# An attention and feed-forward kernel on one core: the first two batches by head pair, dense exponentials, quadrant kv, new weight layout

## The chip, the cores and the metric

The kernel runs on one core of one Trainium2 chip. Spans and instants come from one profiled execution per kernel and count from its first instruction. PE is TensorE (PEld its weight loads), ACT is ScalarE, DVE is VectorE, POOL is GpSimd, SP issues the DMAs.

## The reference

```python
# q, k, v: 8 batches x 8 heads x 576 x 64, f32
q_s = softmax(q, axis=-1)                 # over the 64 dimensions
k_s = softmax(k, axis=2)                  # over the 576 positions
kv  = einsum('bhsd,bhse->bhde', k_s, v)
att = einsum('bhsd,bhde->bhse', q_s, kv)
x   = att.transpose(0, 2, 1, 3).reshape(4608, 512)
h   = x @ w_in                            # 512 x 2048
g   = h * sigmoid(beta * h)
out = g @ w_out                           # 2048 x 512
```

## The kernel before

The work is cut into chunks, one per batch (512 rows) and one for the 64 last rows of all batches. Per chunk there are 16 groups `mm_a(c, j)` of four 128x512 matmuls (first product, followed by tanh on ACT and a multiplication on DVE) and 16 groups `mm_b(c, j)` of four (second product). Attention of a later batch is done beside the products of an earlier one. Batches 0 and 1 are special: batch 0 has nothing to hide behind, and batch 1's inputs come after all weights in the queue of loads. The program fixes the order of instructions on each engine, and each engine works in that order.

For batches 0 and 1 a tile of k holds a head pair, one head on partitions 0 to 63 and one on 64 to 127. `ek` was filled with zeros so that one 128x128 matmul does both heads:

```python
def kz_exp(b, j, m=1):
    for e in range(2):                      # two exps of 64 partitions each
        r = slice(e * D, (e + 1) * D)
        nc.scalar.activation(ek[b][r, j : j + m, :, e * D : (e + 1) * D],
                             k_st[b][r, j : j + m, :]..., ACTF.Exp)
# kv_mm: 9 matmuls per pair
nc.tensor.matmul(t[:, jl, 0:D1], ek[b][:, j, i, :], va[b][:, j, i, :], ...)

load_q(0, parts=2); load_kv(k_st, k, 0, "k_st", parts=4); load_kv(v_st, v, 0, "v_st", parts=4)
nc.sync.dma_start(beta_r[:], ...)
w_load("in", 0, 0); w_load("in", 0, 1); w_load("out", 0, 0); w_load("in", 1); w_load("out", 0, 1)
# ... rest of the weights, q of batch 1, then its k and v

# hand-over from batch 0 to batch 1, as emitted
for u in range(4, NJ):
    mm_a(0, u)                              # with exceptions at 4 and 5, cut
    mm_b(0, u - LAG)
    # ... q_exp, q_sum, q_mul, q_pet(1, 0 and 1) of batch 1 at u = 10 to 13, cut
    if u >= 12:
        kz_exp(1, u - 12)
for j in (2, 3):
    q_pet(1, j, nc.vector)                  # transposes of q on PE, copied out by DVE
mm_b(0, NJ - 2)
kv_mm(1, 0); kv_norm(1, 0)                  # two pairs in one PSUM tile
warm(2)
kv_mm(1, 1); kv_norm(1, 1)
mm_b(0, NJ - 1)
for j in range(HP):
    x_mm(1, j, nc.scalar if j % 2 == 0 else nc.vector, tag="h" if j < 2 else "att")
```

The softmax here doesn't subtract the row's maximum and nothing guards it: scores larger than these inputs give would overflow.

Of the kernel before, what the change touches and what calls it, by code (L numbers as in the profile page):

```python
# [17 lines left out]
def kernel(  # L18
# [40 lines left out]
    beta_r = const.tile([NJ, P], F32, name="beta_r")  # L59
    ident16 = const.tile([NJ, NJ], F32, name="ident16")  # L60
    w_in_b = const.tile([P, KT, FF], BF16, name="w_in_b")
# [11 lines left out]
    w_out_d = moe_w_out.rearrange("(j p) f -> p j f", p=P)  # L73
# [6 lines left out]
    def load_q(b, parts=1):  # L80
        t = stage.tile([P, H, R * D], F32, tag="q_st", bufs=2, name=f"q_st{b}")
        src = q[b, :, 0:MAIN, :].rearrange("h (p i) d -> p h (i d)", i=R)
        n = H // parts
        for s in range(parts):
            nc.sync.dma_start(t[:, s * n : (s + 1) * n, :], src[:, s * n : (s + 1) * n, :])  # L85
        q_st[b] = t
# [12 lines left out]
    def load_kv(d, src, b, tag, parts=1):  # L99
        t = stage.tile([P, H * (R + 1) * D], F32, tag=tag, bufs=2, name=f"{tag}{b}")  # L100
        if b < NW:
            d[b] = t[:, 0 : HP * RW * D].rearrange("p (j r) -> p j r", j=HP)
            sv = src[b].rearrange("(j e) (p i) d -> (e p) j (i d)", e=2, i=RW)
            n = HP // parts
            for s in range(parts):
                nc.sync.dma_start(d[b][:, s * n : (s + 1) * n, :], sv[:, s * n : (s + 1) * n, :])  # L106
# [11 lines left out]
    def w_load(kind, blk, half=None):  # L118
        if (kind, blk) not in wst:
            wst[kind, blk] = stage.tile([P, 4, 512], F32, tag="wo", bufs=4, name=f"w_{kind}{blk}")  # L120
        t = wst[kind, blk]
        if kind == "in":
            src = w_in_d[:, :, ds(blk * 512, 512)]
            c = slice(0, 512) if half is None else slice(half * 256, half * 256 + 256)
            nc.sync.dma_start(t[:, :, c], src[:, :, c])
        else:
            src = w_out_d[:, ds(4 * blk, 4), :]
            c = slice(0, 4) if half is None else slice(half * 2, half * 2 + 2)
            nc.sync.dma_start(t[:, c, :], src[:, c, :])

    def w_cast(kind, blk, half, eng):
        t = wst[kind, blk]
        if kind == "in":
            dst = w_in_b[:, :, ds(blk * 512 + half * 256, 256)]
# [12 lines left out]
    def ek_buf(b, eng=None):  # L147
        t = work.tile([P, HP * RW * P], BF16, tag="ek", bufs=2, name=f"ek{b}")
        if b < NW:
            ek[b] = t[:].rearrange("p (j i m) -> p j i m", j=HP, i=RW)  # L150
            eng.memset(t[:].bitcast(F32), 0.0)
# [3 lines left out]
    def kz_exp(b, j, m=1):  # L155
        for e in range(2):
            r = slice(e * D, (e + 1) * D)
            nc.scalar.activation(  # L158
                ek[b][r, j : j + m, :, e * D : (e + 1) * D],
                k_st[b][r, j : j + m, :].rearrange("p j (i d) -> p j i d", i=RW),  # L160
                ACTF.Exp,
            )
# [65 lines left out]
    def q_mul(b, s, n=2):  # L228
        m = H // n
        h = slice(s * m, (s + 1) * m)  # L230
        nc.vector.tensor_tensor(  # L231
# [25 lines left out]
    def kv_mm(b, jj, n=2, tag="att"):  # L257
        t = ps.tile([P, n, D1 if b < NW or COLT else 2 * D1], F32, tag=tag, bufs=2 if tag == "att" else 1, name=f"kv{b}_{jj}")
        att_of[b, jj] = t
        for jl in range(n):  # L260
            j = n * jj + jl
            if b < NW:
                for i in range(RW):
                    nc.tensor.matmul(  # L264
                        t[:, jl, 0:D1],
                        ek[b][:, j, i, :],
                        va[b][:, j, i, :],
                        start=(i == 0),
                        stop=(i == RW - 1),
                    )  # L270
# [80 lines left out]
    def mm_a(c, j, kts=None, tag=None):  # L351
# [103 lines left out]

    load_q(0, parts=2)
    load_kv(k_st, k, 0, "k_st", parts=4)
    load_kv(v_st, v, 0, "v_st", parts=4)
    nc.sync.dma_start(beta_r[:], moe_beta.rearrange("(j p) -> j p", p=P))
    w_load("in", 0, 0)  # L460
    w_load("in", 0, 1)
    w_load("out", 0, 0)
    w_load("in", 1)
    w_load("out", 0, 1)
    w_load("out", 1)
    w_load("in", 2)
    w_load("out", 2)
    w_load("in", 3)
    load_q(1, parts=2)
    w_load("out", 3, 0)  # L470
    load_kv(k_st, k, 1, "k_st", parts=4)
    w_load("out", 3, 1)
    load_kv(v_st, v, 1, "v_st", parts=2)
# [6 lines left out]
    make_identity(nc, ident16[:])  # L480
    ek_buf(0, nc.vector)
    nc.vector.memset(kvp[:, 0 : B - 1], 0.0)
    v_buf(0)
    ek_buf(1, nc.gpsimd)
# [17 lines left out]
    warm(18)  # L502
    for s in range(2):
        q_exp(0, s)
        q_sum(0, s)
        q_mul(0, s)
    for s in range(2):
        for j in (2 * s, 2 * s + 1):
            q_pet(0, j, nc.vector)
        warm(10 if s == 0 else 2)  # L510
    for j in range(HP):
        kz_exp(0, j)

    tb = ps.tile([P, 512], F32, tag="h", bufs=2, name="tb")

    def attn0(p):
        if 0 < p < 3:
            warm(1, tag="acc3")
        if p % 2 == 0:
            vz_cast(0, p, nc.gpsimd)  # L520
            vz_cast(0, p + 1, nc.gpsimd)
        kv_mm(0, p, n=1, tag=f"acc{p}")
        kv_norm(0, p, n=1)

    for p in range(HP):
        attn0(p)
        if p == 2:
            w_cast("in", 0, 0, nc.gpsimd)
        if p >= 1:
            x_mm(0, p - 1, nc.scalar)  # L530
        if p == 1:
            nc.tensor.transpose(tb[:, 0:NJ], beta_r[:], ident16[:])
            nc.scalar.copy(beta_t[:], tb[:, 0:NJ])
        if p >= 2:
            for j in range(2):
                mm_a(0, j, [p - 2])
    x_mm(0, HP - 1, nc.scalar)
    for kind, blk in (("in", 0), ("out", 0)):
        for half in range(2):
            if (kind, half) not in (("in", 0), ("out", 1)):  # L540
                w_cast(kind, blk, half, nc.gpsimd)
    for kt in (2, 3):
        for j in range(2):
            mm_a(0, j, [kt])
    w_cast("in", 1, 0, nc.vector)
    w_cast("in", 1, 1, nc.gpsimd)
    w_cast("out", 0, 1, nc.gpsimd)
    mm_a(0, 2)
    mm_a(0, 3)
    mm_b(0, 0)  # L550
    mm_b(0, 1)

    def pool_cast(*what):
        for kind, blk in what:
            for half in range(2):
                w_cast(kind, blk, half, nc.gpsimd)
# [6 lines left out]

    tail_zero(0)
    pool_cast(("out", 1), ("in", 2), ("out", 2))
    tail_zero(1)
    pool_cast(("in", 3), ("out", 3))

    for u in range(4, NJ):
        if u != 5:  # L570
            mm_a(0, u)
        if u == 4:
            mm_a(0, 5)
            mm_b(0, 2)
            continue
        if u == 13:
            for j in (0, 1):
                q_pet(1, j, nc.vector)
        mm_b(0, u - LAG)
        if u in (10, 11):  # L580
            q_exp(1, u - 10)
        if u in (10, 12):
            q_sum(1, (u - 10) // 2)
        if u in (11, 13):
            q_mul(1, (u - 11) // 2)
        if u >= 12:
# [12 lines left out]
    for j in range(HP):
        x_mm(1, j, nc.scalar if j % 2 == 0 else nc.vector, tag="h" if j < 2 else "att")  # L600
# [95 lines left out]
```

## Time and profile before

| | before |
|---|---|
| time, median | 289.15 us (288.61 to 289.18, 3 runs) |
| profiled span | 286.8 us |
| PE busy, granted clock | 97%, 1.000 |
| PE's stream of products from | 17.95 us (6 product matmuls done earlier) |
| waits in it up to the next line | 0.79 us, all before 39.02 us |
| end of batch 0's last first-product group | 42.92 us |
| first product of batch 1 | 48.75 us |
| from there to the end | 238.05 us |

The page's second part, each digit a fortieth of the span, shows PE near its limit everywhere but at both ends, at full clock:

```profile
PE   7799999999999999999999999999999999999994
...
PEclk9999999999999999999999999999999999999999
```

PE's timeline at the start (start, us, instruction, count, idle time before and who ended it). The first products (`h`) come two at a time between kv and x until 17.95 us. From there to 42.92 us PE has one gap, of 0.79 us read from start to start, ahead of the transposes of q at 39.02.

```profile
15.24 0.61 PE L358 MATMUL h<-xT,w_in_b 128*128 128x512 bf16 x2 [0.20 <-POOL w_in_b L145]
...
17.95 1.24 PE L358 MATMUL h<-xT,w_in_b 128*128 128x512 bf16 x5 [0.24 <-ACT xT L143]
...
39.02 0.61 PE L250 MATMUL tp<-identity,eq 128*128 128x128 bf16 x8 [0.62 <-ACT ek L158]
```

PE's timeline of the hand-over (start, us, instruction, count). A printed length includes a modelled drain of 0.17 us, so one reads from start to start: a group of four takes 0.863 us.

```profile
42.06 1.03 PE L358 MATMUL h<-xT,w_in_b 128*128 128x512 bf16 x4
42.92 1.03 PE L386 MATMUL acc<-w_out_b,g 128*128 128x512 bf16 x4
43.78 0.61 PE L250 MATMUL tp<-identity,eq 128*128 128x128 bf16 x8
44.23 1.03 PE L386 MATMUL acc<-w_out_b,g 128*128 128x512 bf16 x4
45.25 0.74 PE L264 MATMUL kv<-va,ek 128*128 128x65 bf16 x18
45.83 0.59 PE L450 MATMUL warm<-kvp 128*128 128x512 bf16 x2
46.26 0.74 PE L264 MATMUL kv<-va,ek 128*128 128x65 bf16 x18
46.84 1.03 PE L386 MATMUL acc<-w_out_b,g 128*128 128x512 bf16 x4
47.70 1.03 PE L314 MATMUL x<-qsT,kvp 128*128 128x512 bf16 x4
48.75 0.38 PE L358 MATMUL h<-xT,w_in_b 128*128 128x512 bf16 x1
```

### The profile page before, as it was taken

What the parts mean: (1) busy time and instruction counts of PE and PEld (TensorE: products, weight loads), DVE (VectorE), ACT (ScalarE), POOL (GpSimd) and SP (SyncE); (2) the same over time, 40 slices, a digit from 0 to 9 for tenths busy, and PEclk for the clock granted to TensorE, in tenths of its full rate; (3) what the DMA queues carried; (4) which work ended last, traced back from release to release, by engine and by line L of the source; (5) the groups of instructions that cost most, each with busy time, mean ns of one, the idle gap of its engine ahead of it and who ended that gap; (6) DMA issues with size and microseconds to landing.
All of it is one profiled execution on the core that took longest, in us unless ns stands there. A gap on an engine that the chain in (4) does not pass through costs nothing.

```text
span 286.8 us, 4132 instructions
## 1 busy us (share of the span) xinstructions
PE 277.9 (97%) x1595; PEld 127.7 (45%) x1595; DVE 180.0 (63%) x280; ACT 162.9 (57%) x236; POOL 43.7 (15%) x58
## 2 busy tenths in 40 slices
PE   7799999999999999999999999999999999999994
PEld 2444445444444444444444444444445444444441
DVE  7954597695477457855694469456954695464432
ACT  4763586683496448734773568356835563553341
POOL 4458833300030020001200030003000000000000
PEclk9999999999999999999999999999999999999999
DMA  7999999809933963296319911893270033005004
GB/s 242 377 385 387 371 388 321 280 2 264 280 151 76 313 164 146 46 331 175 127 33 270 269 74 76 194 268 119 115 220 2 1 149 73 0 0 149 0 0 146
DMA packets 56227, 50.08 MB, mean 175 GB/s; under 512 B 26240, under 2 KB 47760, under 8 KB 56208
## 3 DMA queue, kind: packets, MB, share of 16 engines
q1 hardware_dynamic: 56064, 49.56, 55.8%
q8 instruction: 12, 0.20, 0.3%
q10 hardware_dynamic: 144, 0.26, 0.3%
q14 instruction: 7, 0.06, 0.1%
HBM read 36.71 MB, written 9.44 MB: 161 GB/s over the span
## 4 chain that ended last, share of the span: by engine, by line
PE 84%; DMA 11%; SPq 1%; POOL 1%; ACT 1%; issue 0%; DVE 0%; ACTq 0%
PE acc L386 40%; PE h L358 39%; DMA w_in<-in_moe_w_in_dram 6%; DMA k_st<-in_k_dram 5%; PE x L314 2%; PE kv L276 2%; POOL w_in_b L145 1%; PE kv L264 0%; PE tp L250 0%; SPq L85 0%; SPq L106 0%; PE x L318 0%; ACT ek L158 0%; DVE g L370 0%; ACT th L368 0%
## 5 line engine op out<-in xcount | busy, mean ns | idle before, releaser
L368 ACT ACTIVATE th<-h,beta_t 128x512 bf16<-128x512 f32 x144 | 98.5, 687 | 102.6 <-PE h L358 100.7
L370 DVE SCALAR_TENSOR_TENSOR g<-th,h 128x512 bf16<-128x512 bf16 x144 | 97.9, 682 | 92.2 <-ACT th L368 90.7
L358 PE MATMUL h<-xT,w_in_b 128*128 128x512 bf16 x576 | 146.1, 379 | 0.5 <-ACT xT L143 0.2
L386 PE MATMUL acc<-w_out_b,g 128*128 128x512 bf16 x576 | 145.9, 379 | 0.2 <-DVE g L370 0.2
L386 PEld LDWEIGHTS <-g 128*128 128x128 bf16 x576 | 56.0, 98 | 67.9 <-DVE g L370 1.0
L358 PEld LDWEIGHTS <-w_in_b 128*128 128x128 bf16 x576 | 55.3, 98 | 67.7 <-issue 2.7
L145 POOL CAST va<-v_st 128x2048 bf16<-128x2048 f32 (+2 forms) x12 | 17.3, 1460 | 145.0 <-DMA v_st<-in_v_dram 145.0
L225 DVE TENSOR_REDUCE rq<-eq 128x16 f32<-128x1024 bf16 x18 | 21.6, 1198 | 2.3 <-ACT eq L214 2.3
L231 DVE TENSOR_TENSOR eq<-eq,rq 128x1024 bf16<-128x1024 bf16 x18 | 22.6, 1257 | 0.1
L214 ACT ACTIVATE eq<-q_st 128x1024 bf16<-128x1024 f32 x16 | 16.3, 1048 | 2.9 <-DMA q_st<-in_q_dram 2.9
L143 ACT CAST xT<-x 128x512 bf16<-128x512 f32 x20 | 11.6, 585 | 11.1 <-PE x L314 10.3
L169 ACT ACTIVATE ek<-k_st 128x1024 bf16<-128x1024 f32 x12 | 12.6, 1047 | 0.0
L145 DVE COPY o<-acc 128x512 f32<-128x512 f32 x18 | 11.6, 683 | 0.9 <-PE acc L386 0.9
L314 PE MATMUL x<-qsT,kvp 128*128 128x512 bf16 x32 | 11.7, 380 | 0.4 <-DVE kvp L309 0.2
L145 DVE CAST xT<-x 128x512 bf16<-128x512 f32 x16 | 10.9, 684 | 0.5 <-PE x L314 0.5
L143 ACT COPY o<-acc 128x512 f32<-128x512 f32 x18 | 9.7, 591 | 2.6 <-PE acc L386 2.6
L158 ACT ACTIVATE ek<-k_st 64x576 bf16<-64x576 f32 x16 | 10.9, 679 | 0.4
L450 PE MATMUL warm<-kvp 128*128 128x512 bf16 x34 | 9.9, 432 | 1.2 <-DVE kvp L478 1.2
L145 POOL CAST w_out_b<-w_out 128x1024 bf16<-128x1024 f32 x8 | 8.2, 1040 | 6.6 <-DMA w_out<-in_moe_w_out_dram 6.5
L309 DVE TENSOR_TENSOR kvp<-kv,rk 64x256 bf16<-64x256 f32 (+2 forms) x24 | 8.0, 333 | 0.6
L145 POOL CAST w_in_b<-w_in 128x1024 bf16<-128x1024 f32 x7 | 7.2, 1040 | 3.5 <-DMA w_in<-in_moe_w_in_dram 3.4
L450 PEld LDWEIGHTS <-kvp 128*128 128x128 bf16 x34 | 3.4, 108 | 5.3 <-issue 2.1
(38 smaller groups left out, 67.1 us busy)
## 6 DMA issues: line engine op xcount, KB each, us to landing
out_dram<-o SPq DMA_DIRECT2D x14, 512.0 KB, 3.4
q_st<-in_q_dram SPq DMA_DIRECT2D x6, 1024.0 KB, 6.5
k_st<-in_k_dram SPq DMA_DIRECT2D x6, 1024.0 KB, 9.1
v_st<-in_v_dram SPq DMA_DIRECT2D x6, 1024.0 KB, 10.5
w_in<-in_moe_w_in_dram SPq DMA_DIRECT2D x3, 1024.0 KB, 9.7
k_st<-in_k_dram SPq DMA_DIRECT2D x8, 288.0 KB, 7.6
q_st<-in_q_dram SPq DMA_DIRECT2D x4, 512.0 KB, 7.8
w_out<-in_moe_w_out_dram SPq DMA_DIRECT2D x4, 512.0 KB, 9.5
```

Source lines behind the costliest of these rows:

```text
L143: eng.copy(dst, src)
L145: eng.tensor_copy(dst, src)
L169: nc.scalar.activation(ek[b][:, :, h, :].rearrange("p i h d -> p h i d"), k_st[b][:, h, 0 : R * D].rearrange("p h (i d) -> p h i d", i=R), ...
L214: nc.scalar.activation(eq[b][:, :, s * m : (s + 1) * m, :].rearrange("p i h d -> p h i d"), q_st[b][:, s * m : (s + 1) * m, :].rearrange(" ...
L225: nc.vector.tensor_reduce(rq[b][:, 0, :, h], eq[b][:, :, h, :], axis=AX.X, op=ALU.add)
L231: nc.vector.tensor_tensor(eq[b][:, :, h, :], eq[b][:, :, h, :], rq[b][:, 1, :, h].unsqueeze(3).to_broadcast((P, R, m, D)), ALU.mult,)
L314: nc.tensor.matmul(t[:], kvp[:, c, j, :], qsT[c][:, :, j, :])
L358: nc.tensor.matmul(h[:], w_in_b[:, kt, ds(j * P, P)], x_of(c)[:, kt, :], start=(kt == 0), stop=(kt == KT - 1),)
L368: nc.scalar.activation(th[:], h[:], ACTF.Tanh, scale=beta_t[:, j : j + 1])
L370: nc.vector.scalar_tensor_tensor(out=g[:], in0=th[:], scalar=1.0, in1=h[:], op0=ALU.add, op1=ALU.mult)
L386: nc.tensor.matmul(acc[st][:], g[:, ds(st * P, P)], w_out_b[:, j, :], start=(j == 0), stop=(j == NJ - 1),)
L450: nc.tensor.matmul(t[:, 0:cols], kvp[:, B - 1, 0, :], kvp[:, B - 1, :, :].rearrange("p j r -> p (j r)")[:, 0:cols],)
```

## The change

The intent is to begin the products sooner and to thread batch 1's attention between batch 0's last products. k and v are loaded pair by pair; exp(k) is written dense, one instruction of 128 partitions per pair, without zero fill; kv runs as two 64x64 quadrants; w_in lies in eight tiles with its columns interleaved, so that a partition of w_out receives two neighbouring rows, 4 KB, in one run. The order of the start-up, of the loads and of the hand-over is new.

```diff
-    w_out_d = moe_w_out.rearrange("(j p) f -> p j f", p=P)
+    w_out_d = moe_w_out.rearrange("(hh p e) f -> p hh e f", p=P, e=2)
+    w_in_u = [t[:].rearrange("p kt (q e) -> p kt e q", e=2) for t in w_in_b]
 # exp(k): one instruction per pair, no zero fill
+        nc.scalar.activation(ek[b][:, j, :], k_st[b][:, j, :], ACTF.Exp)
 # kv
+                    for e in range(2):
+                        r = slice(e * D, (e + 1) * D)
+                        nc.tensor.matmul(t[r, jl, 0:D1], ek[b][r, j, ds(i * D, D)], va[b][r, j, i, :],
+                                         ..., tile_position=(e * D, e * D))
 # loads
+    for j in range(HP):
+        load_kv(k_st, k, 0, "k_st", [j])
+        load_kv(v_st, v, 0, "v_st", [j])
     w_load("in", 0, 0)
+    nc.sync.dma_start(beta_r[:], ...)          # was ahead of w_in
     w_load("in", 0, 1)
     w_load("out", 0, 0)
+    w_load("out", 0, 1)                         # was behind w_in's block 1
     w_load("in", 1)
 # start-up: ... (cut) its end, before the first product
+    tb = ...; nc.tensor.transpose(... beta_r ...) x2
+    kv_mm(0, 3, n=1, tag="acc3"); kv_norm(0, 3, n=1)
+    x_mm(0, 2, nc.scalar); x_mm(0, 3, nc.scalar)
 # early stream: a0 a1 a2 a3 b0 b1 b2 b3 a4 a5 a6 b4 a7 b5 ...
 # hand-over
+    kz_exp(1, 0)
+    mm_a(0, NJ - 1)
+    kz_exp(1, 1)
+    q_pet(1, 2, nc.scalar); q_pet(1, 3, nc.vector)
+    kv_mm(1, 0, n=1); kv_norm(1, 0, n=1)
+    kz_exp(1, 2)
+    mm_b(0, NJ - 3)
+    kv_mm(1, 1, n=1); kv_norm(1, 1, n=1)
+    x_mm(1, 0, nc.scalar, tag="h")
+    kz_exp(1, 3)
+    mm_b(0, NJ - 2)
+    kv_mm(1, 2, n=1); kv_norm(1, 2, n=1)
+    x_mm(1, 1, nc.vector, tag="h")
+    kv_mm(1, 3, n=1); kv_norm(1, 3, n=1)
+    mm_b(0, NJ - 1)
+    x_mm(1, 2, nc.scalar); x_mm(1, 3, nc.scalar)
```

Also changed: the normalisation of q's last pair goes to GpSimd, and the two zero fills of the tail buffers on GpSimd (1.8 us each) stand elsewhere in its order.

More of the change, by code (lines that the diff above doesn't have):

```diff
@@ L58 @@
     beta_t = const.tile([P, NJ], F32, name="beta_t")
-    beta_r = const.tile([NJ, P], F32, name="beta_r")
-    ident16 = const.tile([NJ, NJ], F32, name="ident16")
-    w_in_b = const.tile([P, KT, FF], BF16, name="w_in_b")
+    beta_r = const.tile([NJ // 2, 2 * P], F32, name="beta_r")
+    ident8 = const.tile([NJ // 2, NJ // 2], F32, name="ident8")
+    w_in_b = [const.tile([P, KT, 2 * P], BF16, name=f"w_in_b{hh}") for hh in range(NJ // 2)]
     w_out_b = const.tile([P, NJ, DM], BF16, name="w_out_b")
@@ L78, with load_q @@
     g_of, acc_of, att_of = {}, {}, {}
-    def load_q(b, parts=1):
-        t = stage.tile([P, H, R * D], F32, tag="q_st", bufs=2, name=f"q_st{b}")
+    def load_q(b, parts=1, only=None):
+        if b not in q_st:
+            q_st[b] = stage.tile([P, H, R * D], F32, tag="q_st", bufs=2, name=f"q_st{b}")
+        t = q_st[b]
         src = q[b, :, 0:MAIN, :].rearrange("h (p i) d -> p h (i d)", i=R)
         n = H // parts
-        for s in range(parts):
+        for s in range(parts) if only is None else (only,):
             nc.sync.dma_start(t[:, s * n : (s + 1) * n, :], src[:, s * n : (s + 1) * n, :])
-        q_st[b] = t
     def load_qtail():
@@ L97, in load_qtail, with load_kv @@
         q_st[B] = t
-    def load_kv(d, src, b, tag, parts=1):
-        t = stage.tile([P, H * (R + 1) * D], F32, tag=tag, bufs=2, name=f"{tag}{b}")
+    kv_st = {}
+    def load_kv(d, src, b, tag, pairs=None):
+        if (tag, b) not in kv_st:
+            kv_st[tag, b] = stage.tile([P, H * (R + 1) * D], F32, tag=tag, bufs=2, name=f"{tag}{b}")
+        t = kv_st[tag, b]
         if b < NW:
@@ L103, in load_kv @@
             sv = src[b].rearrange("(j e) (p i) d -> (e p) j (i d)", e=2, i=RW)
-            n = HP // parts
-            for s in range(parts):
-                nc.sync.dma_start(d[b][:, s * n : (s + 1) * n, :], sv[:, s * n : (s + 1) * n, :])
+            for j in range(HP) if pairs is None else pairs:
+                nc.sync.dma_start(d[b][:, j, :], sv[:, j, :])
         else:
@@ L126, in w_load @@
         else:
-            src = w_out_d[:, ds(4 * blk, 4), :]
-            c = slice(0, 4) if half is None else slice(half * 2, half * 2 + 2)
-            nc.sync.dma_start(t[:, c, :], src[:, c, :])
+            src = w_out_d[:, ds(2 * blk, 2)]
+            c = slice(0, 2) if half is None else slice(half, half + 1)
+            nc.sync.dma_start(t[:].rearrange("p (hh e) f -> p hh e f", e=2)[:, c], src[:, c])
     def w_cast(kind, blk, half, eng):
@@ L133, in w_cast @@
         if kind == "in":
-            dst = w_in_b[:, :, ds(blk * 512 + half * 256, 256)]
+            dst = w_in_b[2 * blk + half][:]
             src = t[:, :, half * 256 : half * 256 + 256]
@@ L145, in evac, with ek_buf, kz_exp @@
             eng.tensor_copy(dst, src)
-    def ek_buf(b, eng=None):
-        t = work.tile([P, HP * RW * P], BF16, tag="ek", bufs=2, name=f"ek{b}")
+    def ek_buf(b):
+        t = work.tile([P, HP * RW * D], BF16, tag="ek", bufs=2, name=f"ek{b}")
         if b < NW:
-            ek[b] = t[:].rearrange("p (j i m) -> p j i m", j=HP, i=RW)
-            eng.memset(t[:].bitcast(F32), 0.0)
+            ek[b] = t[:].rearrange("p (j r) -> p j r", j=HP)
         else:
             ek[b] = t[:, 0 : R * H * D].rearrange("p (i h d) -> p i h d", i=R, h=H)
-    def kz_exp(b, j, m=1):
-        for e in range(2):
-            r = slice(e * D, (e + 1) * D)
-            nc.scalar.activation(
-                ek[b][r, j : j + m, :, e * D : (e + 1) * D],
-                k_st[b][r, j : j + m, :].rearrange("p j (i d) -> p j i d", i=RW),
-                ACTF.Exp,
-            )
+    def kz_exp(b, j):
+        if j == 0:
+            ek_buf(b)
+        nc.scalar.activation(ek[b][:, j, :], k_st[b][:, j, :], ACTF.Exp)
     def k_exp(b, s, n=2):
@@ L226, in q_sum, with q_mul @@
         nc.vector.reciprocal(rq[b][:, 1, :, h], rq[b][:, 0, :, h])
-    def q_mul(b, s, n=2):
+    def q_mul(b, s, n=2, eng=nc.vector):
         m = H // n
         h = slice(s * m, (s + 1) * m)
-        nc.vector.tensor_tensor(
+        eng.tensor_tensor(
             eq[b][:, :, h, :],
@@ L263, in kv_mm @@
                 for i in range(RW):
-                    nc.tensor.matmul(
-                        t[:, jl, 0:D1],
-                        ek[b][:, j, i, :],
-                        va[b][:, j, i, :],
-                        start=(i == 0),
-                        stop=(i == RW - 1),
-                    )
+                    for e in range(2):
+                        r = slice(e * D, (e + 1) * D)
+                        nc.tensor.matmul(
+                            t[r, jl, 0:D1],
+                            ek[b][r, j, ds(i * D, D)],
+                            va[b][r, j, i, :],
+                            start=(i == 0),
+                            stop=(i == RW - 1),
+                            tile_position=(e * D, e * D),
+                        )
                 continue
@@ L359, in mm_a @@
                 h[:],
-                w_in_b[:, kt, ds(j * P, P)],
+                w_in_u[j // 2][:, kt, j % 2, :],
                 x_of(c)[:, kt, :],
@@ L454, in warm @@
             )
-    load_q(0, parts=2)
-    load_kv(k_st, k, 0, "k_st", parts=4)
-    load_kv(v_st, v, 0, "v_st", parts=4)
-    nc.sync.dma_start(beta_r[:], moe_beta.rearrange("(j p) -> j p", p=P))
+    load_q(0, 2)
+    for j in range(HP):
+        load_kv(k_st, k, 0, "k_st", [j])
+        load_kv(v_st, v, 0, "v_st", [j])
     w_load("in", 0, 0)
+    nc.sync.dma_start(beta_r[:], moe_beta.rearrange("(hh q) -> hh q", q=2 * P))
     w_load("in", 0, 1)
     w_load("out", 0, 0)
+    w_load("out", 0, 1)
     w_load("in", 1)
-    w_load("out", 0, 1)
     w_load("out", 1)
@@ L467 @@
     w_load("out", 2)
+    load_q(1, 2, 0)
     w_load("in", 3)
-    load_q(1, parts=2)
-    w_load("out", 3, 0)
-    load_kv(k_st, k, 1, "k_st", parts=4)
-    w_load("out", 3, 1)
-    load_kv(v_st, v, 1, "v_st", parts=2)
+    load_q(1, 2, 1)
+    w_load("out", 3)
+    for j in range(HP):
+        load_kv(k_st, k, 1, "k_st", [j])
+        load_kv(v_st, v, 1, "v_st", [j])
     load_q(2)
@@ L479 @@
     make_identity(nc, identity[:])
-    make_identity(nc, ident16[:])
-    ek_buf(0, nc.vector)
+    make_identity(nc, ident8[:])
     nc.vector.memset(kvp[:, 0 : B - 1], 0.0)
     v_buf(0)
-    ek_buf(1, nc.gpsimd)
     v_buf(1)
@@ L500, in finish_b, with w_cast_kt @@
                 store(c, st)
-    warm(18)
-    for s in range(2):
-        q_exp(0, s)
-        q_sum(0, s)
-        q_mul(0, s)
-    for s in range(2):
-        for j in (2 * s, 2 * s + 1):
-            q_pet(0, j, nc.vector)
-        warm(10 if s == 0 else 2)
-    for j in range(HP):
-        kz_exp(0, j)
-    tb = ps.tile([P, 512], F32, tag="h", bufs=2, name="tb")
-    def attn0(p):
-        if 0 < p < 3:
-            warm(1, tag="acc3")
-        if p % 2 == 0:
-            vz_cast(0, p, nc.gpsimd)
-            vz_cast(0, p + 1, nc.gpsimd)
-        kv_mm(0, p, n=1, tag=f"acc{p}")
-        kv_norm(0, p, n=1)
-    for p in range(HP):
-        attn0(p)
-        if p == 2:
-            w_cast("in", 0, 0, nc.gpsimd)
-        if p >= 1:
-            x_mm(0, p - 1, nc.scalar)
-        if p == 1:
-            nc.tensor.transpose(tb[:, 0:NJ], beta_r[:], ident16[:])
-            nc.scalar.copy(beta_t[:], tb[:, 0:NJ])
-        if p >= 2:
-            for j in range(2):
-                mm_a(0, j, [p - 2])
-    x_mm(0, HP - 1, nc.scalar)
-    for kind, blk in (("in", 0), ("out", 0)):
-        for half in range(2):
-            if (kind, half) not in (("in", 0), ("out", 1)):
-                w_cast(kind, blk, half, nc.gpsimd)
-    for kt in (2, 3):
-        for j in range(2):
-            mm_a(0, j, [kt])
-    w_cast("in", 1, 0, nc.vector)
-    w_cast("in", 1, 1, nc.gpsimd)
-    w_cast("out", 0, 1, nc.gpsimd)
-    mm_a(0, 2)
-    mm_a(0, 3)
-    mm_b(0, 0)
-    mm_b(0, 1)
-    def pool_cast(*what):
-        for kind, blk in what:
-            for half in range(2):
-                w_cast(kind, blk, half, nc.gpsimd)
+    def w_cast_kt(blk, half, kh, eng):
+        c = slice(2 * kh, 2 * kh + 2)
+        evac(eng, w_in_b[2 * blk + half][:, c, :], wst["in", blk][:, c, half * 256 : half * 256 + 256])
     def tail_zero(t):
@@ L562, in tail_zero @@
             nc.gpsimd.memset(vt[t][ds(e * TAIL, TAIL), e, :, D:D1], 2.0)
+    warm(18)
+    q_exp(0, 0)
+    q_sum(0, 0)
+    q_mul(0, 0)
+    q_exp(0, 1)
+    kz_exp(0, 0)
+    vz_cast(0, 0, nc.gpsimd)
+    q_sum(0, 1)
+    warm(5)
+    q_pet(0, 0, nc.scalar)
+    q_pet(0, 1, nc.scalar)
+    kv_mm(0, 0, n=1, tag="acc0")
+    kz_exp(0, 1)
+    vz_cast(0, 1, nc.gpsimd)
+    q_mul(0, 2, n=4)
+    q_mul(0, 3, n=4, eng=nc.gpsimd)
+    warm(3)
+    kv_mm(0, 1, n=1, tag="acc1")
+    kv_norm(0, 0, n=1)
@@ new lines @@
+    kv_norm(0, 1, n=1)
+    kz_exp(0, 2)
+    vz_cast(0, 2, nc.gpsimd)
+    warm(4)
+    q_pet(0, 2, nc.scalar)
+    q_pet(0, 3, nc.vector)
+    x_mm(0, 0, nc.scalar, tag="h")
+    x_mm(0, 1, nc.vector, tag="h")
+    kz_exp(0, 3)
+    vz_cast(0, 3, nc.gpsimd)
+    kv_mm(0, 2, n=1, tag="acc2")
+    kv_norm(0, 2, n=1)
+    tb = ps.tile([P, 512], F32, tag="acc0", bufs=1, name="tb")
+    nc.tensor.transpose(tb[:, 0 : NJ // 2], beta_r[:, 0 : 2 * P : 2], ident8[:])
+    nc.tensor.transpose(tb[:, NJ // 2 : NJ], beta_r[:, 1 : 2 * P : 2], ident8[:])
@@ new lines @@
+    kv_mm(0, 3, n=1, tag="acc3")
+    kv_norm(0, 3, n=1)
+    x_mm(0, 2, nc.scalar)
+    x_mm(0, 3, nc.scalar)
+    nc.scalar.copy(
+        beta_t[:].rearrange("p (hh e) -> p e hh", e=2),
+        tb[:, 0:NJ].rearrange("p (e hh) -> p e hh", e=2),
+    )
+    w_cast_kt(0, 0, 0, nc.gpsimd)
+    w_cast_kt(0, 0, 1, nc.vector)
+    w_cast("in", 0, 1, nc.gpsimd)
+    w_cast("out", 0, 0, nc.gpsimd)
+    w_cast("out", 0, 1, nc.gpsimd)
+    for kt in range(KT):
+        for j in range(2):
+            mm_a(0, j, [kt])
@@ L564 @@
+    mm_a(0, 2)
+    mm_a(0, 3)
+    for j in range(4):
+        mm_b(0, j)
+    w_cast("in", 1, 0, nc.vector)
+    w_cast("in", 1, 1, nc.gpsimd)
+    mm_a(0, 4)
+    mm_a(0, 5)
+    w_cast("out", 1, 0, nc.gpsimd)
+    w_cast("out", 1, 1, nc.gpsimd)
     tail_zero(0)
-    pool_cast(("out", 1), ("in", 2), ("out", 2))
+    w_cast("in", 2, 0, nc.gpsimd)
+    w_cast("in", 2, 1, nc.gpsimd)
+    w_cast("out", 2, 0, nc.gpsimd)
+    w_cast("out", 2, 1, nc.gpsimd)
     tail_zero(1)
-    pool_cast(("in", 3), ("out", 3))
@@ L569 @@
-    for u in range(4, NJ):
-        if u != 5:
-            mm_a(0, u)
-        if u == 4:
-            mm_a(0, 5)
-            mm_b(0, 2)
-            continue
-        if u == 13:
-            for j in (0, 1):
-                q_pet(1, j, nc.vector)
-        mm_b(0, u - LAG)
-        if u in (10, 11):
-            q_exp(1, u - 10)
-        if u in (10, 12):
-            q_sum(1, (u - 10) // 2)
-        if u in (11, 13):
-            q_mul(1, (u - 11) // 2)
-        if u >= 12:
-            kz_exp(1, u - 12)
@@ L588 @@
-    vz_cast(1, 0, nc.gpsimd, m=2)
-    vz_cast(1, 2, nc.gpsimd, m=2)
-    for j in (2, 3):
-        q_pet(1, j, nc.vector)
-    mm_b(0, NJ - 2)
-    kv_mm(1, 0)
-    kv_norm(1, 0)
-    warm(2)
-    kv_mm(1, 1)
-    kv_norm(1, 1)
+    w_cast("in", 3, 0, nc.gpsimd)
+    w_cast("in", 3, 1, nc.gpsimd)
+    w_cast("out", 3, 0, nc.gpsimd)
+    w_cast("out", 3, 1, nc.gpsimd)
+    for j in range(HP):
+        vz_cast(1, j, nc.gpsimd)
+    for u in range(6, NJ - 1):
+        mm_a(0, u)
+        if u in (9, 12):
+            q_exp(1, (u - 9) // 3)
+            q_sum(1, (u - 9) // 3)
+        if u in (10, 13):
+            q_mul(1, (u - 10) // 3)
+        if u == 12:
+            q_pet(1, 0, nc.vector)
+            q_pet(1, 1, nc.vector)
+        mm_b(0, u - 2)
@@ L598 @@
+    kz_exp(1, 0)
+    mm_a(0, NJ - 1)
+    kz_exp(1, 1)
+    q_pet(1, 2, nc.scalar)
+    q_pet(1, 3, nc.vector)
+    kv_mm(1, 0, n=1)
+    kv_norm(1, 0, n=1)
+    kz_exp(1, 2)
+    mm_b(0, NJ - 3)
+    kv_mm(1, 1, n=1)
+    kv_norm(1, 1, n=1)
+    x_mm(1, 0, nc.scalar, tag="h")
+    kz_exp(1, 3)
+    mm_b(0, NJ - 2)
+    kv_mm(1, 2, n=1)
+    kv_norm(1, 2, n=1)
+    x_mm(1, 1, nc.vector, tag="h")
+    kv_mm(1, 3, n=1)
+    kv_norm(1, 3, n=1)
     mm_b(0, NJ - 1)
-    for j in range(HP):
-        x_mm(1, j, nc.scalar if j % 2 == 0 else nc.vector, tag="h" if j < 2 else "att")
+    x_mm(1, 2, nc.scalar)
@@ L601 @@
+    x_mm(1, 3, nc.scalar)
     for st in range(R):
```

## The prediction

> **What bounds the kernel now.** TensorE at full clock (page: PE busy 97%, PEclk 9 throughout). In the timeline 128x512 matmuls follow at 0.863 us per four (216 ns each); from 60 to 270 us PE is never idle. The 1152 matmuls of the two big products need 249 of 286.8 us. The diff touches nothing after batch 1's start but a weight stride, so it can only move when batch 1's dense stream begins: 48.75 us now. Before that PE holds 27.6 us of batch 0's products and about 4 us of attention. PE is gapless only from 17.95 us, with 6 product matmuls (1.3 us) done earlier.
>
> **DMA is the second bound of that stretch.** It moves 365 to 390 GB/s from 5 to 45 us; the chain of waits begins with 32 us of k and w_in transfers. Landings, from who waited: w_in's first half 14.1 us, its block 2 26.9, w_out's block 2 29.7, batch 1's last v about 44.2 (estimate from bytes). The bytes, 15.2 MB, stay.
>
> **What changes.**
> - Dense exp(k): eight 64x576 ACTIVATEs (0.68 us) become four 128x576 of about that time: 2.7 us of ACT saved per batch; two 2 us zero fills go.
> - kv: 36 matmuls at 32 ns become 72 in quadrants. Later batches' column-tiled kv shows 16 ns each, so still 1.2 us per batch (estimate).
> - k, v by pair: pair 0 lands at about 8 us instead of 10.3, the last still at about 12.7. From there: cast 0.8, kv 0.5, normalise 0.7, x 0.4, evacuate 0.6: last xT at about 15.7. w_in's first half is split over POOL and DVE (0.5 instead of 1.04 us): first product at 14.6, gapless from there: 2.0 us earlier than 17.95 minus 1.3.
> - w_out's second half now precedes w_in's block 1, which lands 1.4 us later (about 21.1): a stall of about 0.4 us at j=4. w_out's block 1 (24.2, cast 1.04) stalls that j's second product by about 0.6 us.
> - Batch 1: attention by pair is threaded between batch 0's last products, so the kv burst, two warm matmuls and four x (45.25 to 48.75) shrink; its products start at about 46.6.
> - 4 KB runs of w_out: the weight stretch already runs at 387 GB/s; I count nothing. The interleaved columns of w_in are read at stride 2 in all 576 first products. LDWEIGHTS takes 98 ns of a 216 ns matmul. The Trainium skill ("TensorE: Matmul & The Clock Gate", Fast Weight Load) allows column steps up to 1,024 and gives plain loading as columns/1.2 ns, 107 ns: hidden either way. No run shows one yet.
>
> **Sum.** 2.0 earlier, 1.0 lost to DMA stalls, 1.1 gained at the hand-over: 2.1 us off the critical path; the later 238 us unchanged. Predicted 287.0 us, 285.3 to 288.3; faster 3%, same 94%, slower 3%.
>
> **What would show each step.** Timeline: first product near 14.6, gapless from there; small PE gaps near 22 and 25 us ended by casts of w_in and w_out; kv at 16 ns each; batch 1's first product near 46.6; 60 to 270 us unchanged; LDWEIGHTS of w_in near 98 ns.
>
> **What would make it wrong.** Strided weight loads longer than a matmul (tens of us slower); quadrants serialising or draining PE at each mode change; a cold PE clock early, where warm matmuls fall from 34 to 30; GpSimd's share of q's normalisation (unmeasured) delaying the v casts; DMA faster with longer runs (about 1 us more).

## More of the kernel before

Times are device microseconds (us) of the slowest core, here the only one; quoted times are medians.

PSUM has eight tiles: two `h`, two `att`, four accumulators. The `att` ring of two serves q's transposes, kv and some of the x products.

The busy time by stretch: from 51 to 270 us PE has no idle time; between 15 and 42.9 us DMA runs at 383 GB/s; between 42.9 and 51, which holds the hand-over to batch 1, PE is also full.

```profile
core 0: us, PE busy (x) PEld busy (x) DVE busy (x) ACT busy (x) POOL busy (x), PEclk, DMA share, GB/s
...
15.00:42.90 27.90, 26.73 (x136) 12.13 (x136) 17.14 (x29) 17.20 (x26) 17.90 (x24) 1.00 1.05 383
42.90:51.00 8.10, 8.07 (x73) 4.26 (x72) 6.27 (x15) 4.86 (x9) 2.63 (x3) 1.00 1.11 319
51.00:270.00 219.00, 219.00 (x1255) 100.59 (x1254) 138.49 (x209) 126.03 (x182) 16.03 (x17) 1.00 0.49 142
```

## The result, and the profile after

| | before | after |
|---|---|---|
| time, median | 289.05 us (4 runs) | 290.27 us (289.98 to 291.02, 4 runs) |
| ratio | | 1.0047, 95% interval 1.0033 to 1.0061 |
| profiled span | 286.8 us | 288.6 us |
| PE's stream of products from | 17.95 us, less 1.3 us done before: 16.65 | 16.59 us |
| waits in it up to the next line | 0.79 us, before 39.02 | 0.80 us, before 26.02 |
| end of batch 0's last first-product group | 42.92 us | 42.88 us |
| first product of batch 1 | 48.75 us | 50.59 us |
| from there to the end | 238.05 us | 238.01 us |

The change is 0.5% slower: inside the 2% that the class "same" allows, but clear of noise, and 3.3 us from the predicted 287.0.

The table localises the loss. Up to the end of batch 0's last first product the two kernels are level (0.04 us), after batch 1's first product too (0.04 us). The whole 1.8 us lies in the hand-over, 7.71 us instead of 5.83. The busy time by stretch says the same: in the middle line PE was busy 6.75 of 8.10 us, against 8.07.

```profile
15.00:42.90 27.90, 26.83 (x146) 12.23 (x145) 17.95 (x28) 13.79 (x21) 19.56 (x26) 1.00 1.04 389
42.90:51.00 8.10, 6.75 (x99) 3.45 (x99) 5.38 (x19) 4.22 (x8) 1.43 (x3) 1.00 1.12 299
51.00:270.00 219.00, 219.00 (x1255) 100.80 (x1254) 138.31 (x210) 127.08 (x184) 16.01 (x17) 1.00 0.51 142
```

PE's timeline of the hand-over:

```profile
42.02 1.03 PE L361 MATMUL h<-xT,w_in_b 128*128 128x512 bf16 x4
43.09 0.61 PE L250 MATMUL tp<-identity,eq 128*128 128x128 bf16 x8
44.87 0.48 PE L266 MATMUL kv<-va,ek 64*64 64x65 bf16 x18 [1.16 <-ACT qsT L148]
45.27 1.04 PE L389 MATMUL acc<-w_out_b,g 128*128 128x512 bf16 x4
46.24 0.48 PE L266 MATMUL kv<-va,ek 64*64 64x65 bf16 x18
...
46.88 1.03 PE L389 MATMUL acc<-w_out_b,g 128*128 128x512 bf16 x4
47.83 0.47 PE L266 MATMUL kv<-va,ek 64*64 64x65 bf16 x18
...
48.56 0.48 PE L266 MATMUL kv<-va,ek 64*64 64x65 bf16 x18
48.97 1.04 PE L389 MATMUL acc<-w_out_b,g 128*128 128x512 bf16 x4
49.85 0.90 PE L317 MATMUL x<-qsT,kvp 128*128 128x512 bf16 x2
50.59 0.59 PE L361 MATMUL h<-xT,w_in_b 128*128 128x512 bf16 x2
```

Read start to start, the work is 2.59 + 0.45 + four kv at 0.40 + 0.86 = 5.50 us, practically the 5.49 of before; the waits are 2.2 us instead of 0.34. The largest: after the eight transposes (done about 43.5) PE stands until 44.87 for a copy by ACT that frees the `att` tile. ACT's timeline shows why the copy is late: it stands behind an exponential of k in ACT's order. Pair 3's exponential comes only at 47.56, behind the first x copy, which itself waits 1.68 us for PE:

```profile
43.08 0.69 ACT L371 ACTIVATE th<-h,beta_t 128x512 bf16<-128x512 f32 x1 [0.47 <-PE h L361]
43.66 0.67 ACT L162 ACTIVATE ek<-k_st 128x576 bf16<-128x576 f32 x1
44.24 0.58 ACT L148 COPY qsT<-tp 128x512 bf16<-128x512 bf16 x1
44.70 0.69 ACT L162 ACTIVATE ek<-k_st 128x576 bf16<-128x576 f32 x1
47.08 0.58 ACT L148 CAST xT<-x 128x512 bf16<-128x512 f32 x1 [1.68 <-PE x L317]
47.56 0.69 ACT L162 ACTIVATE ek<-k_st 128x576 bf16<-128x576 f32 x1
```

It was not DMA: GpSimd began to cast the last v of batch 1 at 43.78 us.

The start: PE waits 0.81 us for beta's 8 KB, whose load now follows w_in's; pair 3's kv and both last x products stand behind that in PE's order, and the first product behind those. Then PE is gapless up to the hand-over, except for the 0.80 us before 26.02, where a third first product in a row finds both `h` tiles taken. The gap that the kernel before had ahead of q's transposes is gone (they start at 37.26, right behind a product), so the two kernels are level in spite of this one:

```profile
14.79 0.28 PE L548 MATMUL tb<-ident,beta_r 8*128 8x8 f32 x1 [0.81 <-DMA beta_r<-in_moe_beta_dram]
...
15.12 0.48 PE L266 MATMUL kv<-va,ek 64*64 64x65 bf16 x18
...
16.36 0.39 PE L317 MATMUL x<-qsT,kvp 128*128 128x512 bf16 x1 [0.44 <-DVE kvp L312]
16.59 3.62 PE L361 MATMUL h<-xT,w_in_b 128*128 128x512 bf16 x16
...
26.02 1.02 PE L361 MATMUL h<-xT,w_in_b 128*128 128x512 bf16 x4 [0.64 <-DVE g L373]
```

### The profile page after: what moved, and what is told of

Its sections match the earlier page's. It is cut to its first block, busy times and chain, and to the rows that moved or that the text cites. A ratio compares the mean times of both kernels' runs of the same rounds, so it can differ in the third digit from the quotient of the medians. Undisturbed runs are those within 1.5% of the kernel's fastest.

```text
span 288.6 us, 4270 instructions
## 1 busy us (share of the span) xinstructions
PE 279.4 (97%) x1664; PEld 128.4 (44%) x1664; DVE 177.9 (62%) x282; ACT 159.1 (55%) x232; POOL 42.8 (15%) x60
## 4 chain that ended last, share of the span: by engine, by line
PE 81%; DMA 14%; SPq 2%; POOL 1%; ACT 0%; DVE 0%; issue 0%
PE h L361 39%; PE acc L389 38%; DMA k_st<-in_k_dram 6%; DMA w_out<-in_moe_w_out_dram 4%; DMA v_st<-in_v_dram 4%; PE x L317 2%; PE kv L279 2%; SPq L111 1%; POOL w_out_b L150 1%; SPq L114 0%; SPq L88 0%; PE x L321 0%; POOL vt L510 0%; DVE g L373 0%; ACT th L371 0%
## 5 line engine op out<-in xcount | busy, mean ns | idle before, releaser
L150 POOL CAST va<-v_st 128x576 bf16<-128x576 f32 (+1 forms) x14 | 17.9, 1282 | 151.5 <-DMA v_st<-in_v_dram 151.5
L231 DVE TENSOR_TENSOR eq<-eq,rq 128x1024 bf16<-128x1024 bf16 (+1 forms) x18 | 21.3, 1186 | 0.1
L312 DVE TENSOR_TENSOR kvp<-kv,rk 64x64 bf16<-64x64 f32 (+1 forms) x28 | 8.6, 308 | 0.7
L150 POOL CAST w_in_b<-w_in 128x1024 bf16<-128x1024 f32 (+1 forms) x7 | 6.7, 978 | 3.7 <-DMA w_in<-in_moe_w_in_dram 3.7
L162 ACT ACTIVATE ek<-k_st 128x576 bf16<-128x576 f32 x8 | 5.4, 686 | 0.7 <-DMA k_st<-in_k_dram 0.7
```

The costliest lines, as they stand in the source:

```text
L150: eng.tensor_copy(dst, src)
L231: eng.tensor_tensor(eq[b][:, :, h, :], eq[b][:, :, h, :], rq[b][:, 1, :, h].unsqueeze(3).to_broadcast((P, R, m, D)), ALU.mult,)
```

## The experiments

All are correct. The first theory: the loss lies in waits made by the order of the new hand-over on the engines, and the start-up gained nothing. The rivals: DMA decides the hand-over; or the new instructions (quadrants, strided weights) cost the time.

### e1_old_handover

```diff
-    kz_exp(1, 0) ... the new hand-over ...
+    the hand-over of before, word for word (listed under "The kernel before")
```

> The changed kernel with the earlier kernel's hand-over order put back (k exponentials threaded in from j=12, kv in two tiles of two pairs, the x products in a row, no x or q copy ahead of the k exponentials on ACT). Theory (waits in the program order of the new hand-over: 7.7 us from the end of batch 0's last first product to batch 1's first, against 5.8 us before, though the last v had landed at 43.8 us): about 1.4 us faster than the changed kernel, near 288.8 us, PE idle between 42.9 and 49 us under 0.4 us. Rival 1 (DMA decides the hand-over): unchanged at 290.3. Rival 2 (quadrant kv or stride-2 weights cost the time): unchanged or within 0.3 us.

Measured: 288.99 us, ratio to before 1.0003 (0.9988 to 1.0019). Batch 1's first product came at 48.94 us, 6.13 us after the end of batch 0's last, at 42.81:

```profile
42.81 1.03 PE L389 MATMUL acc<-w_out_b,g 128*128 128x512 bf16 x4
...
48.94 3.29 PE L361 MATMUL h<-xT,w_in_b 128*128 128x512 bf16 x14
```

With the order of the hand-over put back, and loads, quadrants and strides left as the change has them, the kernel is level with the one before. Of the 1.88 us that the hand-over had lost, the order is 1.58 (7.71 less 6.13). The other 0.30 us stay; 0.24 of them are kv in quadrants, two blocks of 0.70 us where two of 0.58 stood. So both rivals fall as the main cause, but the second is right about a small part. The traces of all runs agree: the hand-over takes 7.70 or 7.71 us in each of the six with the new order left alone (the change, e2, e3, e9, e15, e16), and 6.13 or 6.14 in each of the four with the old one and its warm matmuls (e1, e5, e6, e12).

### e4_act_order

```diff
-    kz_exp(1, 1)
     q_pet(1, 2, nc.scalar)
+    kz_exp(1, 1)
     q_pet(1, 3, nc.vector)
     kv_mm(1, 0, n=1); kv_norm(1, 0, n=1)
     kz_exp(1, 2)
+    kz_exp(1, 3)
 ...
     x_mm(1, 0, nc.scalar, tag="h")
-    kz_exp(1, 3)
```

> Only the order of ACT's work in the hand-over: the copy of q's transpose ahead of pair 1's k exponential, and pair 3's k exponential ahead of the first x copy. Theory (in-order ACT holds back PE): the 1.16 us wait of PE for the copy falls to about 0.5, pair 3's exponential at 45.1 to 46 instead of 47.6; 0.7 to 1.2 us faster than the changed kernel, 289.1 to 289.6. Rival (the two buffers of the att ring, not ACT, hold it): under 0.3 us.

Measured: 289.59 us (1.0025, 1.0012 to 1.0038), 0.68 us faster than the changed kernel, at the lower edge of what was expected. PE's wait for the copy fell from 1.16 to 0.79:

```profile
42.64 0.61 PE L250 MATMUL tp<-identity,eq 128*128 128x128 bf16 x8
44.04 0.48 PE L266 MATMUL kv<-va,ek 64*64 64x65 bf16 x18 [0.79 <-ACT qsT L148]
```

That is about half of the 1.28 us that e1 regained, but not all of it comes from the edit: the profiled run of e4 reached the hand-over at 42.62, 0.26 us sooner than the changed kernel. The hand-over itself fell from 7.71 to 7.14 us, so the order on ACT alone is 0.57 of the 1.58 us, about a third. The rest goes with the order on PE: the kv of a pair right behind the transposes, through the same ring of two tiles, with no product between. That part was only tried as a whole, in e1.

### e2_old_start and e12_both_old

e2 puts the start-up of before into the changed kernel, beta's load early as it needs; e12 has both the old start-up and the old hand-over, with the new layout, loads and quadrants.

```diff
-    warm(18); q_exp(0, 0) ... the new start-up ...
+    the start-up of before: q whole, four transposes, k exponentials, then per pair kv, x,
+    and from pair 2 on two first products
```

> The changed kernel with the earlier kernel's start-up order (q whole, then k exponentials, kv and x one pair after the other with the first products between them) and beta's load ahead of w_in as before; hand-over stays new. Theory (the new start-up gained nothing, since its gapless stretch begins at 16.6 us, as the earlier one's 17.95 less 1.3): within 0.5 us of the changed kernel's 290.3. Rival (the new start-up is worth about 2 us, as predicted, and something else ate it): 1.5 us or more slower, 291.8 or more.

> Old start-up and old hand-over, with the new layout, loads (beta early) and early stream. If the two parts act independently: 291.05 less 1.28, about 289.8, so that layout, load order and quadrants alone cost some 0.7 us against the kernel before and the new start-up earns it back. If the start-up's gain is hidden wherever the hand-over doesn't wait: as e1_old_handover, 289.0.

| | old hand-over | new hand-over |
|---|---|---|
| old start-up | 289.57 (e12) | 291.05 (e2) |
| new start-up | 288.99 (e1) | 290.27 (the change) |

Measured: e2 is 1.0069 of before (1.0057 to 1.0081). The 0.78 us between e2 and the change fits neither expectation. "Gained nothing" was too strong, "about 2 us" far too much: by the medians the new start-up is worth 0.78 us beside the new hand-over and 0.58 beside the old one, the new hand-over costs 1.48 and 1.28. The 0.58 alone is not clear of noise (the intervals of e12 and e1 overlap), but the traces say the same: batch 0's last first product ended at 43.65 (e2) and 43.51 us (e12) with the old start-up, at 42.88 (the change) and 42.81 (e1) with the new one. The two parts act nearly independently, e12 lying closer to the 289.8 of that case than to 289.0. e12 is not told apart from the kernel before (1.0008, 0.9983 to 1.0032). The cells are medians from different chips, the medians of the kernel before in these jobs lying between 289.05 and 289.12.

### e3_beta_early

```diff
+    nc.sync.dma_start(beta_r[:], ...)
     w_load("in", 0, 0)
-    nc.sync.dma_start(beta_r[:], ...)
```

> Only beta's 8 KB load goes back ahead of w_in's first half. Theory (PE stood 0.8 us at the transposes of beta, and pair 3's kv was queued behind them): kv of pair 3 from 15.1 to about 14.65, first product from 16.6 to about 16.1, and since the later stages wait for DMA and for ACT, 0.2 to 0.4 us in the total, near 290.0. Rival (the start is set by w_in's landing and its cast): nothing.

Measured: 290.30 us (1.0044, 1.0032 to 1.0056), nothing gained. In this profile the first product came at 15.45 us, 1.14 us sooner than in that of the changed kernel. Not all of this is beta's: with beta late it came at 15.77 in e1, 15.85 in e4 and 16.08 in e8, and e15, a second profile of the changed kernel, has it at 16.56 without a wait for beta. PE's timeline shows where the earlier start went:

```profile
15.45 3.62 PE L361 MATMUL h<-xT,w_in_b 128*128 128x512 bf16 x16
...
29.13 1.04 PE L361 MATMUL h<-xT,w_in_b 128*128 128x512 bf16 x4 [0.55 <-POOL w_in_b L150]
```

In the changed kernel the group at 29.13 began at 29.47: of 1.14 us, 0.34 were left. Another 0.29 went ahead of q's transposes, which begin at 37.20 where PE was free at 36.91, and the end of batch 0's last first product was at 42.82 instead of 42.88. GpSimd's timeline of e3 has the cast of w_in's block 2 only at 28.03, behind zero fills, not waiting for DMA, and the cast of its last block at 33.96, waiting for DMA. The second fence is DVE's multiplication of q that the transposes need:

```profile
24.32 2.03 POOL L150 CAST w_out_b<-w_out 128x1024 bf16<-128x1024 f32 x2 [1.04 <-DMA w_out<-in_moe_w_out_dram]
26.29 0.96 POOL L510 MEMSET vt<- 128x1040 bf16 x1
...
28.03 2.02 POOL L150 CAST w_in_b<-w_in 128x1024 bf16<-128x1024 f32 x2
...
33.96 2.02 POOL L150 CAST w_in_b<-w_in 128x1024 bf16<-128x1024 f32 x2 [0.31 <-DMA w_in<-in_moe_w_in_dram]
```

```profile
35.56 1.49 DVE L231 TENSOR_TENSOR eq<-eq,rq 128x1024 bf16<-128x1024 bf16 x1
```

An earlier start is worth only as much as the arrival of the weights, landed and cast, lets through. Five profiles (the change, e1, e3, e4, e8) begin anywhere from 15.45 to 16.59 us and end batch 0's last first product between 42.62 and 42.88.

### e5_handover_beta, e6_zero_early, e7_no_warm

They build on each other: e5 is e1 with beta early, e6 moves a zero fill, e7 drops two warm matmuls.

```diff
 # e6
+    tail_zero(0)
     w_cast("out", 1, 0, nc.gpsimd)
     w_cast("out", 1, 1, nc.gpsimd)
-    tail_zero(0)
 # e7
     kv_norm(1, 0)
-    warm(2)
     kv_mm(1, 1)
```

> The old hand-over order (as e1_old_handover, 288.99 us) with beta's load early (as e3_beta_early, where the gapless stretch began 1.14 us sooner and the total did not move). Theory (in e3 the gain was swallowed in mid-stream, where GpSimd's zero fills stood ahead of the cast of w_in's block 2 and PE waited 0.55 us for it): as e1 within 0.3 us, 288.7 to 289.1, with PE waiting for that cast near 29 us. Rival (the new hand-over alone swallowed it): 287.9 to 288.2.

> e5 with the first zero fill of the tail buffers moved ahead of the casts of w_out's block 1, where GpSimd waited for DMA anyway. Theory (GpSimd's order sets the cast of w_in's block 2): that cast starts near 27 instead of 28.0 us, PE's eighth first product near 28.4 instead of 29.1, 0.4 to 0.8 us faster than e5, about 288.3. Rival (DMA alone sets it): under 0.2 us.

> e6 without the two warm matmuls in the hand-over (0.43 us of PE). Theory (PE is the bound from there on): 0.3 to 0.45 us faster than e6, about 287.9, which would be the fastest so far and 0.4% faster than the kernel before. Rival (pair 2 and 3's kv is bound by the landing and cast of v, at 44.5 us): nothing.

Measured: e5 289.17 us (0.9995, 0.9981 to 1.0010), as e1, so the new hand-over is not what swallowed the gain. Its profile waits 0.53 us for the cast of w_in's block 2, as the theory has it, and its last cast of w_in, which waits for DMA, came 0.39 us later than in e1 (34.33 against 33.94). e6 288.92 (0.9992, 0.9979 to 1.0004): only 0.25 us less, under what was expected. The cast did move, from 28.45 in e5 to 27.39, and PE's wait for it went; a new one of 0.55 us came at 37.5, for q's normalisation on DVE. e7 288.18 (0.9978, 0.9959 to 0.9997): 0.74 us less, more than the 0.43 us of the warm matmuls. The hand-over of its profile is 5.48 us instead of 6.13, 0.65 less: beside the 0.43, kv now runs in one block (1.29 us instead of twice 0.70). Its profiled run also had its weights cast about 0.5 us sooner than that of e6, which nothing in the edit explains; that is a spread from run to run.

The new wait of e6 and e7 has a cause of its own. The same multiplication of q took 1.92 us in e7 (first line, DVE's timeline), where GpSimd was casting from 33.76 to 35.78, and 1.21 us in the changed kernel (second fence), where GpSimd's cast had ended at 35.66:

```profile
34.94 1.92 DVE L231 TENSOR_TENSOR eq<-eq,rq 128x1024 bf16<-128x1024 bf16 x1
```

```profile
35.90 1.21 DVE L231 TENSOR_TENSOR eq<-eq,rq 128x1024 bf16<-128x1024 bf16 x1
```

The Trainium skill ("SBUF — State Buffer", section "Who interferes with whom") says that a VectorE instruction with two SBUF inputs contends with a GpSimd instruction that reads SBUF. This trace agrees.

All the traces, looked at together, make more of it. In ten of them (e1, e3 to e9, e15, e16) the multiplication starts during the cast of w_in's last block. It then ends 1.07 or 1.08 us after the end of that cast, whether it had begun 0.34 us (e15) or 0.84 us (e7) before it, and PE's transposes follow 0.14 or 0.15 us later. So in these kernels the cast, which waits for DMA, sets when PE reaches the hand-over, and PE's own start does not; that is where the earlier start of e3 ended. The kernel before shows it too: its multiplication began at 36.95, during a cast of w_out that ended at 37.80, took 1.93 us and ended at 38.88. In the changed kernel, e2 and e12 the multiplication began after the cast and took 1.21 us.

### e8_quadrant_order

```diff
-                for i in range(RW):
-                    for e in range(2):
+                for e in range(2):
+                    for i in range(RW):
```

> Only a measurement: the changed kernel with the two quadrants of a pair one after the other (nine matmuls at partitions 0 to 63, then nine at 64 to 127) instead of alternating. If the two quadrants overlap when alternated, 18 matmuls now take longer than the 0.40 us start to start of the changed kernel, toward 0.5 to 0.6 us. If each costs a fixed 22 ns whatever its place, 0.40 us again.

Measured (one look, of unknown state, so its 290.73 us is not used): 18 matmuls of a pair took 0.59 us from the start of kv to that of the next instruction, against 0.40 when the two quadrants alternate:

```profile
44.61 0.66 PE L266 MATMUL kv<-va,ek 64*64 64x65 bf16 x18 [1.35 <-ACT qsT L148]
45.20 1.04 PE L389 MATMUL acc<-w_out_b,g 128*128 128x512 bf16 x4
```

Alternated quadrants overlap, as the Trainium skill says ("TensorEngine Tiling (Array Packing)", Key Properties: tiles operate independently). The same section says that changing the tiling mode drains the engine. Lengths of alternated kv fit that: 18 in a row take 0.40 us, 36 in e1 0.70, 72 in e7 about 1.29. That is 16.5 ns per matmul plus about 0.10 us per block, whereas the 128x128 kv of before took 0.29 us for 9 and 0.58 for 18, no fixed part. The drain itself is not seen in a trace; the fixed part is worked out, and that it is the drain is not shown.

### e9_contiguous and e16_contiguous_again (with e15_after_again)

```diff
-    w_out_d = moe_w_out.rearrange("(hh p e) f -> p hh e f", p=P, e=2)
-    ... "p kt (q e) -> p kt e q"
+    w_out_d = moe_w_out.rearrange("(hh e p) f -> p hh e f", p=P, e=2)
+    ... "p kt (e q) -> p kt e q"
```

(beta's columns follow.) e15 is the changed kernel itself.

> The changed kernel with w_out in 2 KB runs and w_in's weights at stride 1, as in the kernel before, all else new. As predicted (neither matters): 290.3 within 0.3 us, LDWEIGHTS of w_in 98 ns as with stride 2. Rival (4 KB runs speed the weight stretch): 0.4 us or more slower, weight blocks landing later. Rival (stride 2 costs PE): faster.

> The changed kernel again, as the reference of the next run on the same chip: 290.3.

> e9_contiguous again beside the changed kernel. If the 4 KB runs are worth something: 0.4 to 0.7 us slower than e15_after_again, the last v of batch 1 cast more than 1 us later, 382 against 391 GB/s from 15 to 40 us. If it was the chip: the same time.

Measured: e9 290.87 us (1.0064, 1.0050 to 1.0079). On one chip, e15 290.65 (1.0053, 1.0023 to 1.0083) and e16 291.18 (1.0065, 1.0037 to 1.0093). So 0.5 to 0.6 us in favour of the 4 KB runs both times, but the intervals overlap. From 15 to 40 us both traces with 2 KB runs show 382 GB/s, those with 4 KB runs 390 or 391. The expected sign on v failed: its last cast began at 44.51 us in e16 and 44.62 in e15, as that profiled run of e16 was also ahead at the start. LDWEIGHTS of w_in has a median of 98 ns in both layouts, so the stride costs nothing that the trace shows.

### e10_q_earlier, e11_w_in_first, e13_both_repairs

e10 is e7 with batch 1's q steps at j = 8, 9, 11, 12 instead of 9, 10, 12, 13 and its last two transposes ahead of `mm_b(0, 13)`. e11 is e10, and e13 is e7, with this (the casts of these weights follow the new order, cut here):

```diff
-    w_load("out", 0, 1)
     w_load("in", 1)
+    w_load("out", 0, 1)
 ...
-    for j in range(4):
+    for j in range(2):
         mm_b(0, j)
     mm_a(0, 4)
     mm_a(0, 5)
+    for j in range(2, 4):
+        mm_b(0, j)
```

> e7 (288.18 us) with batch 1's q work one step earlier and its last two transposes ahead of the thirteenth second product. Theory (what is left are waits of PE for q's normalisation, 0.55 us at 37 us, and for the transposes' copies, 0.4 us at 44.9 us): both go, 0.6 to 1.0 us faster than e7, 287.2 to 287.6. Rival (the start of batch 1 is bound by the landing of v, and PE then waits there instead): under 0.3 us.

> e10 with w_in's block 1 loaded ahead of w_out's second half, as in the kernel before, and two second products before it. Theory (the new order of loads made PE wait at j=4, near 22.5 to 25 us, as predicted): 0.3 to 0.5 us faster than e10. Rival (later blocks bound it anyway): as e10 within 0.2 us.

> e7_no_warm with w_in's block 1 first (which gave 0.35 us on e10_q_earlier). If PE's waits add up: 287.8, 0.4% faster than before. If DMA's later blocks bound the stretch: 288.2 as e7.

Measured: e10 289.00 us (0.9991, 0.9976 to 1.0007), no gain on e7, and slower in ratio, though the intervals overlap: the wait at the transposes became one of 0.51 us just before, where a first product waits for a vector operation. DVE's two q multiplications of batch 1 had both fallen beside GpSimd casts, 1.88 and 1.90 us. The hand-over, 5.48 us in both profiles, got no shorter: the 0.4 us wait read out of e7 was one of the weight loads, while PE, start to start, had stood 0.1 us. That expectation rested on a misreading.

e11 288.65 (0.9979, 0.9965 to 0.9993), 0.35 us less than e10, the size expected, but the intervals overlap, and its profile does not show the cause: PE waits 0.96 us for w_in's cast before 22.66. e13 287.91 us (0.9954, 0.9927 to 0.9981) is the fastest of all: 0.46% under the kernel before, and beside 290.65 for the changed kernel on the same chip 0.9% under that (medians). Its edits together: old hand-over without its warm matmuls, beta early, zero fill early, w_in's block 1 first, all on the new layout. The last of these is not shown to help: e13's interval overlaps that of e7, and in the profiles its thirteenth first product began at 35.50 us, that of e7 at 35.42. What e13's profile gains comes next: there the multiplication of q took 1.23 us and the cast beside it 3.02, where in e7 it was 1.92 and 2.02, so PE's transposes began at 36.40 instead of 37.00. Which of the two gets ahead of the other was not planned; that is luck. Its hand-over, 5.91 us, is longer than e7's 5.48.

## Why the prediction was wrong

It foresaw 2.1 us gained and 1.8 were lost in the trace, 3.9 us apart. They fall into two steps.

- **"2.0 earlier, 1.0 lost to DMA stalls"**: at the end of batch 0's last first product this should have left 1.0 us; it left 0.04 (0.06 us earlier at the start, a new gap of 0.80, and an old one of 0.79 gone, which the prediction had not seen). "First product at 14.6, gapless from there" was 16.59. The prediction followed data (landing, cast, kv, x) and left out that PE takes beta's transposes and all four x before the first product. The old start-up put back cost 0.58 and 0.78 us: that is what the new one is worth, not 2.0. The deeper fault is that a start 1.14 us sooner in the profile still gained nothing (e3): the step took time saved at the start as time off the total, where PE later waits for casts of w_in and for the multiplication of q that such a cast holds up.
- **"Small PE gaps near 22 and 25 us ended by casts of w_in and w_out"**: the size was nearly right, 0.80 us for 1.0, by luck, as the cause named was not. One gap, before 26.02, ended by the vector operation that freed an `h` tile. That the loads' order matters there is not shown: e11 and e13, which undo it, are 0.35 and 0.27 us faster than e10 and e7, inside the noise.
- **"1.1 gained at the hand-over"**: this is the step that failed most. It lost 1.88 us (7.71 against 5.83), 2.98 us from the prediction. The prediction counted the work that pairing would spread out and assumed that threaded work fills gaps. There had been almost none to fill: 0.34 us. The new order made 2.2 us of waits, through the ring of two `att` tiles and through ACT's order. e1, which undid only this, regained 1.28 us of the time and 1.58 us of the hand-over in the trace; by e4, ACT's order is 0.57 of that.
- **Quadrants at 16 ns each**: 16.5 ns plus 0.10 us per block, so 0.40 us per pair instead of 0.29. Four blocks cost a batch 0.44 us more than before (1.60 against 1.16); one block, as in e7, about 0.13.
- **4 KB runs, "I count nothing"**: about 2% more bandwidth, perhaps 0.5 us. A small miss in the other direction.
- **Right**: the later 238 us unchanged; the stride harmless; DMA as the second bound before batch 1; PE's clock not an issue early (PEclk 9 in every slice but the last).

Open: how the rest of the hand-over's loss divides between the ring and the order on PE; the exact worth of the 4 KB runs; and what shifts the first landings from run to run (the first cast of w_in began at 14.55 us in one profile of the changed kernel and at 15.29 in the other, e15).

## What to carry to other kernels

Threading work into a stretch can gain at most the waiting that is in it: count that first (here 0.34 of 5.83 us), then check for each threaded piece which ring of tiles and which in-order queue it stands in. A gain at the start is worth what the next paced resource lets through, so follow it up to the next wait before counting it; here that was a vector multiplication held up by a GpSimd cast. An 8 KB load or a zero fill can hold a whole engine if its consumer stands early in an in-order queue.

## What the Trainium skill lacked or had wrong

- "TensorEngine Tiling (Array Packing)", Key Properties, says that a mode switch drains TensorE but gives no size for it. Here a block of quadrant kv carries about 0.10 us beyond 16.5 ns per matmul (18, 36 and 72 in 0.40, 0.70 and 1.29 us).
- "TensorE: Matmul & The Clock Gate", Fast Weight Load, allows strided columns without a measured time. Here stride 2 and stride 1 both show 98 ns per LDWEIGHTS of 128 columns.
- "SBUF — State Buffer", Who interferes with whom, was right; it gives no duration for this pair of instructions. Here a VectorE multiplication of 128x1024 took 1.92 us where it began inside a GpSimd cast and 1.21 us after one; in eleven traces it ended 1.07 or 1.08 us after the cast's end, and in e13 it took 1.23 us and two casts 3.02 instead of 2.02.
- "DMA: Bandwidth & Descriptors", Bandwidth, has a table by size of transfer, none by length of the run on the sequencer-issued path of trn2. Here a stretch of mixed loads moved 382 GB/s with w_out in 2 KB runs and 390 or 391 with 4 KB.
